# Fewer bytes from HBM, 16 more GpSimd copies: blocks of k doubled on the chip in a fused window-attention and MoE kernel

## Chip, cores and metric

The kernel runs on one core of one Trainium2 chip. The metric is device time in microseconds (us) for one launch; "profiled execution" is one launch that the hardware profiler recorded, and times inside it count from the start of its span.

## What is computed

```python
# attention: B, H, S, D = 8, 8, 576, 64; every token sees itself and the 63 tokens before it
scores = q @ k.transpose(0, 1, 3, 2) / sqrt(D)
scores = where((rel >= 0) & (rel < 64), scores, -1e9)        # rel = query position - key position
attn = softmax(scores, axis=-1)
x = (attn @ v)                                               # to N, D = 4608, 512
# MoE on x: E = 8 experts, F = 1024, only tokens with x @ w_skip > 0
gate_w, e = max, argmax of softmax(x @ w_gate)
out = x + gate_w * (relu(x @ w1[e]) @ w2[e])                 # other tokens: out = x
```

All arrays are f32.

## The kernel before

A sequence of 576 tokens is nine blocks of 64. A query block needs two key blocks: its own and the one before it. The work is cut into 36 tiles of 128 tokens, and a tile is two query blocks. For each pair m of batches (m = 0 to 3) there are nine tiles: eight with blocks 0 to 7 of the two batches, and as the ninth the "tail" tile 9m+8, the last blocks (block 8) of both batches.

Loads come in groups n = 0 to 15. A group is four blocks (two tiles) of one batch, g = n % 2 says which half of the batch. `first_of[n]` is the group's first tile (0, 2, 4, 6, 9, 11, 13, 15, 18, ...). k lies in four buffers `ks[n % 4]` of five blocks: slots 1 to 4 hold the group's blocks, slot 0 the block before the first one. In an even group slot 0 is zero, set once; in an odd group it is the last block of group n-1, and L209 loads it from HBM again, so that this transfer has five blocks. A tail tile has k tiles `kt` and q tiles `qt` of its own, loaded by `load_qk_tail` (L212) in four transfers, among them block 7 a second time (`kT[..., 7:9]`). v comes in two forms: `vT` for the router's logits, and `vm`, whose four blocks have two halves of partitions: the lower 64 partitions hold the block before, the upper 64 the block itself, or the other way round. `load_vm` (L298) fills every second block over all partitions, GpSimd (L356) and ScalarE (L363, L376) copy the other halves.

The main loop (L1163) is written out by hand under a manual schedule: every engine gets its instructions in the order of the program text. Iteration t does, in this order:

- what the table `at[t]` lists: loads on SP's queue with the memsets that belong to them on GpSimd (L305);
- `score(t+1)` on TensorE: four mask matmuls (L237) and 32 matmuls with q and k (L251), for a tail tile with `qt` and `kt`;
- the gate steps: `gate_v` (L335) and `gate_vt` with GpSimd's copy L356;
- `routes(1)`: one step of the router for a group of tiles (8, 8, 6, 6, 8 tiles). The steps for the first 28 tiles run on GpSimd: `pool_part` (L467 to L504), the ranks (L536 to L538), `one_hots` (L584 to L610), and when the third group is in, `close_first` (L625 to L648);
- softmax of tile t on VectorE (L270, L271) and ScalarE (L276);
- `tile_out(t-2)`: 32 matmuls with v on TensorE (L387), the division on VectorE (L398 to L406), and the store of tile t-4 on SP's queue (L425, L427). x has four buffers;
- two more `routes(1)`, between them the transposes of tile t-1 (L284).

`at[t]` is filled from L1142 on: first for all n (`load_qk` at `first_of[n]-5`, `load_v` at `first_of[n]-4`), then for all m (`load_qk_tail` at 9m+4, `load_v_tail` at 9m+2). So the tail tile 17 of m = 1 is scored in iteration 16, and the tail tile 26 of m = 2 in iteration 25. After the loop come the experts (L911 to L913), whose weights are split by ScalarE (L843) and VectorE (L847).

Of the kernel before, what the change touches and what calls it, by code (L numbers as in the profile page):

```python
# [8 lines left out]
F32 = mybir.dt.float32  # L9
# [9 lines left out]
B, H, S, HD = 8, 8, 576, 64  # L19
N, D, E, F = 4608, 512, 8, 1024  # L20
P = 128
# [27 lines left out]
NQB, NKB, NVB, NTB, NSB, NPB, XPB = 4, 4, 4, 2, 2, 3, 4  # L49
# [20 lines left out]
VW = 64 + 1 + 9  # L70
# [73 lines left out]
def window_attention_moe(ctx: ExitStack, tc, a, out):  # L144
    nc = tc.nc
# [42 lines left out]
    vp = attn.enter_context(tc.tile_pool(name="vp", bufs=2, side="right"))  # L188
# [4 lines left out]
    qkp = scoring.enter_context(tc.tile_pool(name="qkp", bufs=1))  # L193
# [3 lines left out]
    ks = [qkp.tile([P, 5, 4, 64], F32, name=f"k{s}") for s in range(NKB)]  # L197
    for k in ks[::2]:
        nc.gpsimd.memset(k[:, 0], 0.0)
    qs, tails = {}, {}  # L200

    def load_qk(n, parts=((0, 4),), other=nc.sync):
        b, g = divmod(n, 2)
        if parts[0][0] == 0:
            qs[n] = qkp.tile([P, 4, 4, 64], F32, name="q", bufs=NQB)
        q, k = qs[n], ks[n % NKB]
        for s, e in parts:
            s0 = s + 1 if s or not g else 0
            nc.sync.dma_start(k[:, s0 : e + 1], a["kT"][b, :, 4 * g + s0 - 1 : 4 * g + e])  # L209
            other.dma_start(q[:, s:e], a["qT"][b, :, 4 * g + s : 4 * g + e])  # L210

    def load_qk_tail(m):  # L212

        q = qkp.tile([P, 2, 4, 64], F32, name="qt")
        k = qkp.tile([P, 2, 2, 4, 64], F32, name="kt")
        for z in range(2):
            nc.sync.dma_start(k[:, z], a["kT"][2 * m + z, :, 7:9])
            nc.sync.dma_start(q[:, z], a["qT"][2 * m + z, :, 8])
        tails[m] = q, k

    def windows(t):

        m, r = divmod(t, 9)
        if r == 8:
            q, k = tails[m]
            return [(q[:, z], k[:, z]) for z in range(2)]
        n, j = 4 * m + r // 2, 2 * (r % 2)
        return [(qs[n][:, j + z], ks[n % NKB][:, j + z : j + z + 2]) for z in range(2)]

# [58 lines left out]
    ss, pts, vs = {}, {}, {}  # L288
    banks = {}
    vms = {}  # L290

    def load_vT(n):
        b, g = divmod(n, 2)
        vT = vtp.tile([P, 4, 256], F32, name="vT")
        nc.sync.dma_start(vT, a["vT"][b, g])
        vTs[n] = vT

    def load_vm(n, by=nc.sync):  # L298
        b, g = divmod(n, 2)
        vm = vp.tile([P, 4, H, VW], F32, name="vm", bufs=NVB)  # L300
        by.dma_start(
            vm.rearrange("p (j z) h c -> p j z (h c)", z=2)[:, :, 1], a["vp"][b, :, 2 * g : 2 * g + 2]
        )
        if g == 0:
            nc.gpsimd.memset(vm[:64, 0], 0.0)  # L305
        vms[n] = vm

    def load_v(n):
        load_vT(n)
        load_vm(n)  # L310
# [3 lines left out]
    def load_v_tail(m):  # L314
        vt = vp.tile([P, 2, H, VW], F32, name="vt", bufs=1)
        vT = vtp.tile([P, 4, P], F32, name="vTt", bufs=1)
        nc.sync.dma_start(vT, a["vTt"][m])
        for z in range(2):
            nc.sync.dma_start(vt[64:, z], a["vpt"][m, z])
        vms["t", m] = vt, vT  # L320

    def keep_busy(n):
# [17 lines left out]
    def gate_t(vw, nt):  # L340
        pk = psum.tile([P, nt, P], F32, name="pk", tag="t", bufs=2, padded_shape=[P, 4, P])
        for j in range(nt):
            nc.tensor.transpose(pk[:, j], vw[:, j * P : j * P + P], ident)
        return pk.rearrange("p n (h c) -> p n h c", c=16)[..., 0:9]
# [4 lines left out]
    def gate_vt(n):  # L349

        b, g = divmod(n, 2)
        vm = vms[n]
        pg = gate_t(vws.pop(n), 2)
        w = vm.rearrange("p (j z) h c -> p j z h c", z=2)
        nc.scalar.copy(w[:, :, 1, :, 65:74], pg)  # L355
        nc.gpsimd.tensor_copy(w[64:, :, 0], w[:64, :, 1])  # L356
        for j in range(2):
            vs[9 * (n // 4) + 2 * (n % 4) + j] = [vm[:, 2 * j], vm[:, 2 * j + 1]]

    def lower(n, j):  # L360

        before = vms[n][64:, 1] if j else vms[n - 1][64:, 3]
        nc.scalar.copy(vms[n][:64, 2 * j], before)  # L363

    def gate_tail(m):
        vms["t", m] = vms["t", m][0], gate(vms["t", m][1], 1)
# [6 lines left out]
        vs[9 * m + 8] = [vt[:, 0], vt[:, 1]]  # L373

    def tail_lower(m, z):
        nc.scalar.copy(vms["t", m][0][:64, z], vms[4 * m + 2 * z + 1][64:, 3])  # L376

    def av_tile(t, lh, sums, av=None):
        blks = tiles[t]
# [739 lines left out]
    first_of = [9 * (n // 4) + 2 * (n % 4) for n in range(NG)]  # L1119
    with tc.manual_schedule():  # L1120
        other = nc.scalar
        nc.vector.memset(onesb, 1.0)
        nc.sync.dma_start(identb, a["c_identb"])
        other.dma_start(band, a["c_band"])
        load_qk(0, ((0, 2),), other)
        load_qk(0, ((2, 4),), other)
        load_vT(0)
        other.dma_start(ident, a["c_ident"])
        other.dma_start(wg, a["wg"])
        nc.scalar.activation(sm.tile([P, 1], F32, name="warm", bufs=1), onesb[:, 0:1], AF.Exp)  # L1130
        load_qk(1, ((0, 2),), other)
        load_vm(0, other)
        load_qk(1, ((2, 4),), other)
        load_vT(1)
        load_vm(1)
        at = {}

        def when_at(t, f, n):
            at.setdefault(max(t, 0), []).append((f, n))

        gate_at, lower_at = {}, {}
        for n in range(NG):  # L1142
            if n >= 2:
                when_at(first_of[n] - AHEADQ, load_qk, n)
                when_at(first_of[n] - AHEADV, load_v, n)
            gt = max(first_of[n] - (1 if n < NSLOW else 2), 0)
            gate_at.setdefault(gt, []).append((gate_v, n))
            at_t = gt + 1
            gate_at.setdefault(at_t, []).append((gate_vt, n))
            lower_at.setdefault(at_t, []).append((lower, n, 1))  # L1150
            if n % 2:
                lower_at.setdefault(at_t + 1, []).append((lower, n, 0))
        for m in range(B // 2):
            when_at(9 * m + 4, load_qk_tail, m)
            when_at(9 * m + 2, load_v_tail, m)
            lower_at.setdefault(9 * m + 4, []).append((tail_lower, m, 0))
            lower_at.setdefault(9 * m + 7, []).append((tail_lower, m, 1))
            gate_at.setdefault(9 * m + 5, []).append((gate_tail, m))
            gate_at.setdefault(9 * m + 6, []).append((gate_tail_t, m))
# [3 lines left out]
        for t in range(NT - 1):  # L1163
            m, r = divmod(t, 9)
# [206 lines left out]
        while True:  # L1371
            k = place[0]
# [16 lines left out]
    with tc.If(more > 0):  # L1389
        with tc.For_i(0, more, 1) as i:  # L1390
# [15 lines left out]
            for qi in range(NQ):  # L1406
                both = []
                for w in range(2):
                    n = 2 * qi + w
# [15 lines left out]
def layout(inputs):  # L1425
    q, k, v = (np.asarray(inputs[n]) for n in "qkv")
    arr = {}
    for name, z in (("qT", q), ("kT", k)):
        z = z.reshape(B, 4, 2, NB, 64, HD)
        arr[name] = z.transpose(0, 2, 5, 3, 1, 4).reshape(B, P, NB, 4, 64)  # L1430
    vp = np.zeros((B, NB, 64, H, VW), np.float32)
    vp[..., HD] = 1.0
    vp[..., :HD] = v.reshape(B, H, NB, 64, HD).transpose(0, 2, 3, 1, 4)
    arr["vp"] = vp[:, :8].reshape(B, 4, P, H * VW).transpose(0, 2, 1, 3)
    arr["vpt"] = vp[:, 8].reshape(B // 2, 2, 64, H, VW)
    vb = v.reshape(B, 4, 2, S, HD).transpose(0, 2, 4, 1, 3).reshape(B, P, 4, S)
    arr["vT"] = vb[..., :512].reshape(B, P, 4, 2, 256).transpose(0, 3, 1, 2, 4)
    arr["vTt"] = vb[..., 512:].reshape(B // 2, 2, P, 4, 64).transpose(0, 2, 3, 1, 4).reshape(B // 2, P, 4, P)
    wg = np.zeros((2, HD, 4, 2, 16), np.float32)
    for z in range(2):  # L1440
        wg[z, :, :, z, :E] = inputs["moe_w_gate"].reshape(4, 2, HD, E)[:, z].transpose(1, 0, 2)
        wg[z, :, :, z, E] = inputs["moe_w_skip"].reshape(4, 2, HD)[:, z].T
    arr["wg"] = wg.reshape(P, 4, 32)
    w1 = inputs["moe_w1"].reshape(E, NDC, P, NQ, FQ).transpose(0, 3, 2, 1, 4).reshape(E, NQ, P, NDC * FQ)
    w2 = inputs["moe_w2"].reshape(E, NQ, 2, P, D).transpose(0, 1, 3, 2, 4).reshape(E, NQ, P, 2 * D)
    arr["wq"] = np.concatenate([w1, w2], 3).reshape(E * NQ * P, 2048)
    arr.update(constants())
    return {n: np.ascontiguousarray(x) for n, x in arr.items()}
# [17 lines left out]
```

## Time and profile before

| | |
|---|---|
| time, median of 3 (lowest, highest) | 418.26 us (417.87, 418.77) |
| profiled execution | 418.07 us |
| its span (the rest lies around it) | 416.3 us |
| TensorE (PE) busy, matmuls | 398.2 us, 96% |
| VectorE (DVE) busy | 291.6 us, 70% |
| ScalarE (ACT) busy | 219.4 us, 53% |
| GpSimd (POOL) busy | 157.6 us, 38% |
| DMA | 105.73 MB, mean 254 GB/s |

Attention fills the span to about 160 us, the experts the rest. A busy share is a mean over both: which engine holds up the others is read from the waits in a stretch. "[2.10 <-DMA q<-qT]" at the end of a line means that the engine was idle for 2.10 us before this instruction and that the q transfer ended last of what it waited for. PEclk is the clock granted to TensorE as a share of 2.4 GHz, so that 0.50 is the lower level of 1.2 GHz.

### The profile page before, as it was taken

The page shows a single profiled execution, that of the slowest core. Times are in us where ns is not written, and L with a number is a line of the kernel's source. Part 1 is how long each engine was busy: PE and PEld are TensorE (multiplying, and loading weights), DVE is VectorE, ACT ScalarE, POOL GpSimd, SP SyncE. Part 2 cuts the span into 40 slices and gives each one's busy share as a digit, 9 for nine tenths or more (in the row PEclk, how much of TensorE's full clock was granted, in tenths as well). Part 3 has the DMA queues.
Part 4 walks back from the last instruction along what each step waited for, and adds up shares of the span by engine and source line. Part 5 has one row for each costly group of instructions (what it writes and reads, how often), then busy time and mean ns, then how long its engine had stood idle before and what let it go on. Part 6 is the DMA issues. An engine that isn't in the chain of part 4 may idle for free.

```text
span 416.3 us, 11734 instructions
## 1 busy us (share of the span) xinstructions
PE 398.2 (96%) x4687; PEld 334.5 (80%) x4687; DVE 291.6 (70%) x515; ACT 219.4 (53%) x389; POOL 157.6 (38%) x296
## 2 busy tenths in 40 slices
PE   8699999999999889899999999999999999999994
PEld 3587887878778678779988898898888889988873
DVE  3387899899799797999436679555556485656661
ACT  2477868767767695436224436234426355444540
POOL 1431168666958878557103115013016030100110
PEclk9999999999999999899999999999999999999999
DMA  8999999999995695636928937545388866667810
GB/s 296 406 326 375 408 368 382 410 386 310 366 413 195 204 362 173 196 128 219 311 82 254 324 117 258 183 161 205 117 250 291 264 206 202 221 203 244 265 55 23
DMA packets 38554, 105.73 MB, mean 254 GB/s; under 512 B 4864, under 2 KB 6272, under 8 KB 38496
## 3 DMA queue, kind: packets, MB, share of 16 engines
q1 hardware_dynamic: 34016, 93.51, 65.3%
q0 software_dynamic: 3200, 9.58, 6.5%
q10 hardware_dynamic: 1280, 1.85, 1.2%
q8 instruction: 38, 0.62, 0.6%
q14 instruction: 20, 0.16, 0.1%
HBM read 90.86 MB, written 14.39 MB: 253 GB/s over the span
## 4 chain that ended last, share of the span: by engine, by line
PE 68%; DMA 10%; issue 7%; DVE 7%; POOL 4%; ACT 2%; POOLq 0%; ACTq 0%; DVEq 0%
PE av L387 8%; PE p L911 7%; PE p L912 7%; PE p L913 7%; PE pt L284 6%; PE ps L251 5%; DMA out<-yo,les 5%; PE yv L911 3%; PE yw L911 3%; PE yw L912 3%; PE yw L913 3%; PE yv L912 3%; PE yv L913 3%; DMA q<-qT 2%; PE ps L237 2%
## 5 line engine op out<-in xcount | busy, mean ns | idle before, releaser
L847 DVE TENSOR_TENSOR wlo<-raw,whi 128x1024 fp32r<-128x1024 f32 x70 | 85.6, 1233 | 17.5 <-ACT whi L843 17.5
L957 ACT ACTIVATE hh<-p 128x256 fp32r<-128x256 f32 (+6 forms) x72 | 27.7, 384 | 127.3 <-PE p L913 123.0
L911 PE MATMUL p<-xh,whi 128*128 128x256 f32 (+6 forms) x288 | 85.9, 298 | 0.2 <-DVE hl L960 0.2
L912 PE MATMUL p<-xl,whi 128*128 128x256 f32 (+6 forms) x288 | 84.3, 293 | 0.8 <-DVE xl L892 0.8
L913 PE MATMUL p<-xh,wlo 128*128 128x256 f32 (+6 forms) x288 | 84.4, 293 | 0.6 <-DVE wlo L847 0.6
L843 ACT CAST whi<-raw 128x1024 fp32r<-128x1024 f32 x72 | 74.3, 1046 | 0.0
L1003 POOL DMA_INDIRECT out<-yo,les x18 | 17.6, 976 | 147.3 <-DVE yo L994 137.6
L960 DVE SCALAR_TENSOR_TENSOR hl<-p,hh 128x256 fp32r<-128x256 f32 (+6 forms) x72 | 30.1, 419 | 61.2 <-ACT hh L957 35.5
L911 PEld LDWEIGHTS p<-xh,whi 128*128 128x128 f32 x288 | 55.2, 192 | 3.7 <-issue 1.7
L912 PEld LDWEIGHTS p<-xl,whi 128*128 128x128 f32 x288 | 55.3, 192 | 2.1 <-DVE xl L892 1.1
L913 PEld LDWEIGHTS p<-xh,wlo 128*128 128x128 f32 x288 | 55.4, 192 | 0.8 <-DVE wlo L847 0.8
L276 ACT ACTIVATE s<-s 128x1024 f32<-128x1024 f32 x36 | 38.1, 1058 | 30.9 <-DVE s L271 30.8
L270 DVE TENSOR_REDUCE mx<-ps 128x8 f32<-128x1024 f32 x36 | 43.6, 1210 | 6.1 <-PE ps L251 6.1
L271 DVE TENSOR_TENSOR s<-ps,mx 128x1024 f32<-128x1024 f32 x36 | 44.1, 1225 | 4.6
L387 PEld LDWEIGHTS av<-vm,ptm 128*64 128x64 f32 x992 | 35.2, 138 | 12.2 <-issue 5.5
L387 PE MATMUL av<-vm,ptm 128*64 128x74 f32 x992 | 40.4, 233 | 3.4 <-POOL vm L356 1.4
L285 ACT COPY ptm<-pt 128x512 f32<-128x512 f32 x72 | 38.3, 581 | 5.9 <-PE pt L284 5.8
L284 PE MATMUL pt<-ident,s 128*128 128x128 f32 x288 | 39.9, 283 | 0.0
L251 PE MATMUL ps<-k,q 64*64 64x128 f32 x1024 | 33.6, 270 | 2.5 <-DMA q<-qT 2.5
L251 PEld LDWEIGHTS ps<-k,q 64*64 64x64 f32 x1024 | 30.0, 133 | 5.3 <-issue 3.1
L284 PEld LDWEIGHTS pt<-ident,s 128*128 128x128 f32 x288 | 31.6, 143 | 2.5 <-issue 0.3
L356 POOL COPY vm<-vm 64x1184 f32<-64x1184 f32 x16 | 18.6, 1166 | 34.9 <-ACT vm L355 29.2
(225 smaller groups left out, 699.9 us busy)
## 6 DMA issues: line engine op xcount, KB each, us to landing
raw<-wq SPq DMA_DIRECT2D x72, 512.0 KB, 4.7
vm<-vp SPq DMA_DIRECT2D x15, 592.0 KB, 9.1
vT<-vT SPq DMA_DIRECT2D x16, 512.0 KB, 8.3
out<-x SPq DMA_DIRECT2D x32, 256.0 KB, 7.3
q<-qT SPq DMA_DIRECT2D x14, 512.0 KB, 9.1
wr<-wq SPq DMA_DIRECT2D x24, 256.0 KB, 5.5
k<-kT SPq DMA_DIRECT2D x7, 640.0 KB, 8.6
k<-kT SPq DMA_DIRECT2D x7, 512.0 KB, 8.7
```

What stands on the lines that cost most here:

```text
L251: nc.tensor.matmul(ps[64 * hf : 64 * hf + 64, r, p], q[h, p], k[h, :, p], start=False, stop=p == 3, skip_group_check=True,)
L270: nc.vector.tensor_reduce(mx, flat, axis=AX.X, op=ALU.max)
L271: pace[0] = nc.vector.tensor_tensor(s, flat, mx.unsqueeze(2).to_broadcast([P, 8, P]), op=ALU.subtract)
L276: nc.scalar.activation(s, s, AF.Exp, scale=0.125)
L284: nc.tensor.transpose(pt[:, p], s[:, 4 * r + p], ident)
L285: nc.scalar.copy(ptm[:, 4 * r : 4 * r + 4], pt)
L387: nc.tensor.matmul(av[64 * hf : 64 * hf + 64, h // 4, (h % 4) * VW : (h % 4 + 1) * VW], ptm[:, (h % 2) * 4 + h // 2, 64 * hf : 64 * hf + 6 ...
L843: nc.scalar.copy(ring[n % RING][0], raws[n % NRAW])
L847: by.tensor_tensor(lo, raws[n % NRAW], hi.bitcast(F32), op=ALU.subtract)
L911: nc.tensor.matmul(o, lh, rh, start=first, stop=False, skip_group_check=parts)
L912: nc.tensor.matmul(o, lh, rl, start=False, stop=False, skip_group_check=parts)
L913: nc.tensor.matmul(o, ll, rh, start=False, stop=last, skip_group_check=parts)
```

## The change

The blocks of q and k are no longer loaded twice. `kT` and `qT` hold blocks 0 to 7 only. A k transfer has four blocks for every group. Slot 0 of an odd group is copied by GpSimd from slot 4 of group n-1 (`last_block`, 128 x 256 f32, eight copies: one before the loop, seven from `at[first_of[n]-4]`). A tail tile gets one transfer of 512 KB with k and q of both last blocks into a tile of three parts, and GpSimd copies the two block-7 parts from `ks` (`last_block_tail`, 128 x 256 f32, eight copies: in `at[9m+4]` for group 4m+1 and in `at[9m+5]` for group 4m+3). They are entered after all n, so they stand behind the memset of the same iteration. `vm` is laid out by parity: the loaded blocks lie side by side, so a row of the transfer is one run of 4736 bytes in place of two of 2368. The two `vpt` transfers of a tail are one.

```diff
-            s0 = s + 1 if s or not g else 0
-            nc.sync.dma_start(k[:, s0 : e + 1], a["kT"][b, :, 4 * g + s0 - 1 : 4 * g + e])
+            nc.sync.dma_start(k[:, s + 1 : e + 1], a["kT"][b, :, 4 * g + s : 4 * g + e])
...
-        for z in range(2):
-            nc.sync.dma_start(k[:, z], a["kT"][2 * m + z, :, 7:9])
-            nc.sync.dma_start(q[:, z], a["qT"][2 * m + z, :, 8])
-        tails[m] = q, k
+        both = qkp.tile([P, 3, 2, 4, 64], F32, name="kqt")
+        nc.sync.dma_start(both[:, 1:3], a["kqt"][m])
+        tails[m] = both
+
+    def last_block(n):
+        nc.gpsimd.tensor_copy(ks[n % NKB][:, 0], ks[(n - 1) % NKB][:, 4])
+
+    def last_block_tail(n):
+        nc.gpsimd.tensor_copy(tails[n // 4][:, 0, n % 4 // 2], ks[n % NKB][:, 4])
...
-            return [(q[:, z], k[:, z]) for z in range(2)]
+            return [(tails[m][:, 2, z], tails[m][:, 0:2, z]) for z in range(2)]
...
-        vm = vp.tile([P, 4, H, VW], F32, name="vm", bufs=NVB)
+        vm = vp.tile([P, 2, 2, H, VW], F32, name="vm", bufs=NVB)
...
-        for z in range(2):
-            nc.sync.dma_start(vt[64:, z], a["vpt"][m, z])
+        nc.sync.dma_start(vt[64:], a["vpt"][m])
...
-        nc.gpsimd.tensor_copy(w[64:, :, 0], w[:64, :, 1])
+        nc.gpsimd.tensor_copy(vm[64:, 0], vm[:64, 1])
...
         load_qk(1, ((2, 4),), other)
+        last_block(1)
...
                 when_at(first_of[n] - AHEADV, load_v, n)
+                if n % 2:
+                    when_at(first_of[n] - 4, last_block, n)
...
             when_at(9 * m + 4, load_qk_tail, m)
+            when_at(9 * m + 4, last_block_tail, 4 * m + 1)
+            when_at(9 * m + 5, last_block_tail, 4 * m + 3)
```

## Rows read from the trace of the kernel before

**Rows 1.** Busy us and count of each engine in a stretch: PE, PEld, DVE, ACT, POOL.
```profile
60.00:80.00 20.00, 20.00 (x434) 16.00 (x422) 18.27 (x34) 15.61 (x29) 16.03 (x35) 1.00 1.03 379
```

**Rows 2.** The chain that ended last, in order of time: start, us, what.
```profile
8.23 8.80 DMA q<-qT
...
75.31 0.87 PE ps L251 x32
...
137.98 1.17 POOL vm L356
```

**Rows 3.** Timeline, TensorE: start, us, line, out<-in, [idle before <-releaser].
```profile
17.17 0.56 PE L251 MATMUL ps<-k,q 64*64 64x128 f32 x12 [2.10 <-DMA q<-qT]
```

**Rows 4.** DMA issues: queue, count, KB each, median us from issue to landing.
```profile
vm<-vp ACTq DMA_DIRECT2D x1, 592.0 KB, 9.0
k<-kT SPq DMA_DIRECT2D x1, 384.0 KB, 6.3
```

**Rows 5.** Windows as in rows 1; the last three columns: PEclk, DMA share, GB/s.
```profile
14.00:18.00 4.00, 1.85 (x44) 1.13 (x44) 0.47 (x1) 1.27 (x4) 1.96 (x3) 1.00 1.04 411
18.00:22.00 4.00, 4.00 (x53) 3.51 (x45) 1.24 (x5) 1.62 (x3) 3.94 (x9) 0.60 1.03 408
136.00:140.00 4.00, 2.57 (x68) 1.84 (x70) 2.64 (x4) 3.15 (x6) 3.78 (x6) 1.00 0.41 121
168.00:172.00 4.00, 2.00 (x18) 1.08 (x17) 4.00 (x10) 1.22 (x2) 1.47 (x2) 1.00 0.63 194
172.00:176.00 4.00, 3.96 (x20) 3.96 (x21) 3.36 (x12) 1.68 (x3) 1.76 (x8) 0.57 0.60 179
```

**Rows 6.** Timeline, GpSimd, its first long run without idle time.
```profile
67.65 0.20 POOL L591 CAST vals<-gl 128x8 bf16<-128x8 f32 x1
67.80 0.62 POOL L598 TENSOR_TENSOR xg<-cf,gc 128x256 f32<-128x256 f32 x1
...
73.97 2.47 POOL L610 TENSOR_TENSOR xg<-xg,vals 128x640 bf16<-128x640 f32 x2
76.39 0.58 POOL L305 MEMSET vm<- 64x592 f32 x1
77.03 1.17 POOL L356 COPY vm<-vm 64x1184 f32<-64x1184 f32 x1
```

**Rows 7.** Timeline, TensorE: the scores of tail tiles 17 and 26.
```profile
75.14 1.04 PE L251 MATMUL ps<-kt,qt 64*64 64x128 f32 x32
...
111.15 0.50 PE L251 MATMUL ps<-kt,qt 64*64 64x128 f32 x12
```

**Rows 8.** Timeline, GpSimd: small one-input instructions.
```profile
32.01 0.29 POOL L179 CAST trib<-cf 128x128 bf16<-128x128 f32 x1 [1.80 <-DMA cf<-c_f]
32.24 0.19 POOL L180 COPY base<-cf 128x8 f32<-128x8 f32 x1
```

**Rows 9.** Timeline, GpSimd: its second long run, and the idle time after it.
```profile
95.86 0.30 POOL L536 TENSOR_TENSOR gds<-gds,gohb 128x64 f32<-128x64 f32 x1 [2.01 <-DVE gds L529]
...
109.79 0.59 POOL L305 MEMSET vm<- 64x592 f32 x1
...
112.85 0.28 POOL L468 TENSOR_TENSOR lg<-lh 128x54 f32<-128x54 f32 x1
...
117.46 0.27 POOL L498 TENSOR_TENSOR goh<-gfi,gfm 128x48 f32<-128x48 f32 x1 [2.39 <-DVE gfm L492]
```

**Rows 10.** Timeline, VectorE, behind that run.
```profile
113.17 0.20 DVE L481 TENSOR_REDUCE gmx<-lg 128x6 f32<-128x48 f32 x1 [1.84 <-POOL lg L468]
```

**Rows 11.** Timeline, SP's queue: a k load and the store behind it.
```profile
102.90 0.92 SPq L209 DMA_DIRECT2D k<-kT  x1
...
104.54 0.45 SPq L425 DMA_DIRECT2D out<-x  x1
```

**Rows 12.** Timeline, the experts' stage: VectorE and GpSimd at the same time.
```profile
175.67 2.36 DVE L847 TENSOR_TENSOR wlo<-raw,whi 128x1024 fp32r<-128x1024 f32 x2
...
175.96 1.07 POOL L586 TENSOR_SCALAR gc<-gc 128x8 f32<-128x8 f32 x1
```

More of the change, by code (lines that the diff above doesn't have):

```diff
@@ L207, in load_qk @@
         for s, e in parts:
-            s0 = s + 1 if s or not g else 0
-            nc.sync.dma_start(k[:, s0 : e + 1], a["kT"][b, :, 4 * g + s0 - 1 : 4 * g + e])
+            nc.sync.dma_start(k[:, s + 1 : e + 1], a["kT"][b, :, 4 * g + s : 4 * g + e])
             other.dma_start(q[:, s:e], a["qT"][b, :, 4 * g + s : 4 * g + e])
     def load_qk_tail(m):
-        q = qkp.tile([P, 2, 4, 64], F32, name="qt")
-        k = qkp.tile([P, 2, 2, 4, 64], F32, name="kt")
-        for z in range(2):
-            nc.sync.dma_start(k[:, z], a["kT"][2 * m + z, :, 7:9])
-            nc.sync.dma_start(q[:, z], a["qT"][2 * m + z, :, 8])
-        tails[m] = q, k
+        both = qkp.tile([P, 3, 2, 4, 64], F32, name="kqt")
[5 more added lines that the diff above has]
+        nc.gpsimd.tensor_copy(tails[n // 4][:, 0, n % 4 // 2], ks[n % NKB][:, 4])
     def windows(t):
@@ L224, in windows @@
         if r == 8:
-            q, k = tails[m]
-            return [(q[:, z], k[:, z]) for z in range(2)]
+            return [(tails[m][:, 2, z], tails[m][:, 0:2, z]) for z in range(2)]
         n, j = 4 * m + r // 2, 2 * (r % 2)
@@ L299, in load_vm @@
         b, g = divmod(n, 2)
-        vm = vp.tile([P, 4, H, VW], F32, name="vm", bufs=NVB)
+        vm = vp.tile([P, 2, 2, H, VW], F32, name="vm", bufs=NVB)
         by.dma_start(
-            vm.rearrange("p (j z) h c -> p j z (h c)", z=2)[:, :, 1], a["vp"][b, :, 2 * g : 2 * g + 2]
+            vm[:, 1].rearrange("p j h c -> p (j h c)"),
+            a["vp"][b, :, 2 * g : 2 * g + 2].rearrange("p j c -> p (j c)"),
         )
         if g == 0:
-            nc.gpsimd.memset(vm[:64, 0], 0.0)
+            nc.gpsimd.memset(vm[:64, 0, 0], 0.0)
         vms[n] = vm
@@ L353, in gate_vt @@
         pg = gate_t(vws.pop(n), 2)
-        w = vm.rearrange("p (j z) h c -> p j z h c", z=2)
-        nc.scalar.copy(w[:, :, 1, :, 65:74], pg)
-        nc.gpsimd.tensor_copy(w[64:, :, 0], w[:64, :, 1])
+        nc.scalar.copy(vm[:, 1, :, :, 65:74], pg)
+        nc.gpsimd.tensor_copy(vm[64:, 0], vm[:64, 1])
         for j in range(2):
-            vs[9 * (n // 4) + 2 * (n % 4) + j] = [vm[:, 2 * j], vm[:, 2 * j + 1]]
+            vs[9 * (n // 4) + 2 * (n % 4) + j] = [vm[:, 0, j], vm[:, 1, j]]
     def lower(n, j):
-        before = vms[n][64:, 1] if j else vms[n - 1][64:, 3]
-        nc.scalar.copy(vms[n][:64, 2 * j], before)
+        before = vms[n][64:, 1, 0] if j else vms[n - 1][64:, 1, 1]
+        nc.scalar.copy(vms[n][:64, 0, j], before)
     def gate_tail(m):
@@ L375, in tail_lower @@
     def tail_lower(m, z):
-        nc.scalar.copy(vms["t", m][0][:64, z], vms[4 * m + 2 * z + 1][64:, 3])
+        nc.scalar.copy(vms["t", m][0][:64, z], vms[4 * m + 2 * z + 1][64:, 1, 1])
     def av_tile(t, lh, sums, av=None):
@@ L1430, in layout @@
         arr[name] = z.transpose(0, 2, 5, 3, 1, 4).reshape(B, P, NB, 4, 64)
+    last = np.stack([arr[name][:, :, 8] for name in ("kT", "qT")], 2)
+    arr["kqt"] = last.reshape(B // 2, 2, P, 2, 4, 64).transpose(0, 2, 3, 1, 4, 5)
+    for name in ("qT", "kT"):
+        arr[name] = arr[name][:, :, :8]
     vp = np.zeros((B, NB, 64, H, VW), np.float32)
@@ L1434, in layout @@
     arr["vp"] = vp[:, :8].reshape(B, 4, P, H * VW).transpose(0, 2, 1, 3)
-    arr["vpt"] = vp[:, 8].reshape(B // 2, 2, 64, H, VW)
+    arr["vpt"] = vp[:, 8].reshape(B // 2, 2, 64, H, VW).transpose(0, 2, 1, 3, 4)
     vb = v.reshape(B, 4, 2, S, HD).transpose(0, 2, 4, 1, 3).reshape(B, P, 4, S)
```

## The prediction, made before the changed kernel ran

> **What bounds the kernel now.** I read the stretches first, then the chain, then the queues of the engines that the change touches. In the middle of attention TensorE is busy without a gap (20.00 of 20 us), VectorE nearly so (18.27), GpSimd 16.03 [rows 1]. The chain agrees: it starts with a q transfer, runs over TensorE from 17 to 114 us, then over VectorE and, from 121 to 139 us, over GpSimd, whose copy of v at 137.98 releases TensorE [rows 2]. So bytes matter only at the start, TensorE's own time matters up to 114 us, and GpSimd's queue where it is late. The list of waits between 20 and 114 us has no transfer that TensorE, VectorE or ScalarE waited for.
>
> GpSimd is late twice. The memset at 76.39 belongs to iteration 14 (group 8) and waits for nothing, yet it stands right behind the router's work of iteration 13 [rows 6], while TensorE scores tile 17, which is iteration 16, at 75.14 [rows 7]. So GpSimd works its queue in the order of the text, some two iterations behind TensorE. The second time it has no idle time from 95.86 to 113.13 (112.85 + 0.28): the memset of iteration 23 stands at 109.79 [rows 9], TensorE scores tile 26 (iteration 25) at 111.15 [rows 7], and VectorE sits idle for 1.84 us until GpSimd's `lg` is there [rows 10].
>
> **The change part by part.** The sum is made against the profiled execution's 418.07 us (span 416.3, 1.8 around it). It lies 0.19 below the median of 418.26, inside the spread of 0.9, so I leave the sum as it is.
>
> *Bytes at the start.* k of group 1's first half shrinks from 384 to 256 KB [rows 4]. The transfers run at 411 GB/s with the DMA engines full [rows 5], so what queues behind lands 131 KB / 411 = 0.32 us earlier, and TensorE's wait of 2.10 us for q [rows 3] shrinks by as much: **-0.3**. Bounds: 0 (the transfers on ScalarE's queue don't pass on what SP's saves) and -2.1 (the wait goes altogether).
>
> *Other transfers.* Seven k loads lose 128 KB each, the tails 1 MB in all, and sixteen fewer DMAs are issued. All of it lies under TensorE's unbroken work [rows 1] and nobody waits for it: 0. Without that cover it would be some 2 MB / 411 = 5 us of DMA time. The longer runs of `vm` move the same bytes, and GpSimd copies as many elements as before in L356: 0; at the end of a long run of GpSimd a slower L356 would cost its own difference.
>
> *Price of one copy.* 128 x 256 f32 is not in the trace. One-input instructions take 0.19 for 8 elements a partition, 0.29 for 128 [rows 8], 1.17 for 1184 [rows 6]. The line from 8 to 1184 gives 0.19 + 248 x 0.83 ns = 0.40, and it goes through the point at 128. Bounds: 0.29 (half the elements) and 0.62 (two inputs, 128 x 256, L598 [rows 6]). From start to start add up to 0.07 (0.64 for the memset of 0.58 at 76.39 [rows 6]): 0.43.
>
> *Tail copies of m = 1.* `last_block_tail(5)` is in `at[13]`: in GpSimd's order between L591 (iteration 12) at 67.65 and L598 at 67.80, so all behind it shifts by 0.43. `last_block_tail(7)` is in `at[14]` behind the memset: it starts at 76.39 + 0.43 + 0.64 = 77.46 and ends at 77.86. Tile 17's matmuls with the second half's window need it, the third of the 32 first, at about 75.2 [rows 7]. TensorE's queue is in order: behind the waiting matmul stand the gate, AV of tile 14 and the transposes, and VectorE and ScalarE wait for these. The stretch has no gap that takes it up, so **+2.7** (77.86 + 0.04 for the hand-over - 75.2). Bounds by the copy's: 2.5 to 3.1. Both sides move alike when TensorE is earlier, since GpSimd's run began with VectorE's result of iteration 12.
>
> *The clock behind that wait.* With TensorE busy for 1.85 us of 14 to 18 its granted clock was 0.60 in the next 4 us, and with 2.00 of 168 to 172 it was 0.57, stretches at the lower of the two levels in both; with 2.57 of 136 to 140 it stayed [rows 5]. From 74 to 78 there would be 1.3 us of work. I take a drop: 4 x 0.40 = 1.6 or 4 x 0.43 = 1.7, **+1.7**, on the engine that bounds this stretch. Bounds 0 and 2.0.
>
> *Tail copies of m = 2.* `at[22]` and `at[23]` put two copies around the memset at 109.79, in a run without idle time whose end VectorE awaits [rows 9, 10]: `lg` is later by 2 x 0.43 to 0.47, **+0.9** (bounds 0.6 to 1.3). VectorE runs without a pause from 113.17 to 121.2, hands over to GpSimd's next run, and that ends in the copy at 137.98 on the chain [rows 2]. TensorE's own wait for the second copy is small (109.79 + 0.43 + 0.64 + 0.40 = 111.26 against 111.2 [rows 7]) and not the one that ends last.
>
> *The other copies of `last_block`.* Each has three iterations (some 12 us) before its score. Those of iterations 20 and 25 fall before the idle 2.01 and 2.39 us of [rows 9]; the one of iteration 29 and the tail copies of 31 and 32 stand behind the copy at 137.98, and their readers (scores of tiles 33 and 35) are over 2 us later. I take 0; if the run from 142 to 169 us passes them on, up to +0.5. At the start the copy waits for the second half of group 0's k, with only a memset behind it.
>
> *New waits on SP's queue.* The load of group 13's k (buffer 1, `at[24]`), issued at 102.90 [rows 11], overwrites what `last_block_tail(9)` reads, so it now waits for GpSimd until 109.79 + 0.40 = 110.2. The q load, a store, vT and vm queue behind it for 7.3 us. The store at 104.54 [rows 11] frees the x buffer that VectorE fills again at 120.2; issued at 111.5 and landed 7.3 us later (the median of these stores) it is there at 118.8. vT of group 13 would be there at about 119, its gate is at 121.6. Hidden, with 1.4 to 2.6 us to spare: 0, and if not, up to +3.
>
> Sum: -0.3 + 2.7 + 1.7 + 0.9 = +5.0, so 418.07 + 5.0 = **423.1 us**.
>
> **The rivals.**
> *No drop of the clock* (0.15): as above without 1.7: 421.4. For it: the stall is one piece, and TensorE is fully busy on both sides. Against: less work in the 4 us than before either drop [rows 5].
> *The start gives back more* (0.06). vm of group 0 (592 KB on ScalarE's queue, landed after 9.0 us [rows 4]) has half as many runs now. If queues take turns run by run, q behind it lands some 1 us earlier, 14 to 18 us is busier and the clock stays up there: -1.1 - 1.6 in place of -0.3, 420.7. The Trainium skill, "DMA: Bandwidth & Descriptors", section "Queues, rings and completion order", says that a DMA engine goes round the queues packet by packet; by that rule alone q gains this only if SP's runs beside it don't grow too, and SP's vm, which shares those turns, does grow. The landing times before (vm 15.5, q 17.0, SP's vm 16.5) don't decide it.
> *GpSimd's copies are slowed by VectorE* (0.04). In the experts' stage an instruction on 8 elements a partition took 1.07 us beside L847 [rows 12], where a copy of that size took 0.19 [rows 8]. If the tail copies were slowed by as much (0.9 each), the wait grows by 1.8 and the second run by 1.8: 426.7. Against: the L356 copies took 1.16 to 1.17 us all sixteen times in attention. The Trainium skill, "GPSIMD Engine Reference", section "Key points", says that GpSimd shares its interfaces with VectorE and contends with instructions of two SBUF inputs; L847 is one, attention's large ones read PSUM, so by the rule too the copies stay at their price.
> *SP's stall is not covered* (0.07). It decides as soon as landing takes over 9 us or the copy of iteration 22 is over 1.4 us later than worked out: VectorE then waits for x, up to 3 us: 426.
> *Not slower* (0.08): the tail copies are in time. The point from which it decides is 75.2 us: `last_block_tail(7)` must stand before the run of [rows 6], where its input has long landed, that is, the order of the text must not hold on GpSimd, or the run must be 2.7 us shorter. Then the second run takes them likewise, and the start alone is left: 417.8; with more from the start 416. Against: the memset at 76.39, which had nothing to wait for.
>
> **How the numbers follow.** Forecast (stall, drop, second run) 0.60, and the rivals as given. The predicted time is the forecast's, 423.1. Its own range is 422.1 to 424.6. The range reaches down over "no drop" and "the start gives more" with their bounds, 420.0, and up over part of SP's stall, 425.8; left out are "not slower" and most of the two upper rivals, under 0.2. A measurement of this kernel can tell about 0.2% (0.84 us) from no change. Faster (below 417.4) only in a part of "not slower": 0.03; same 0.06; slower 0.91.
>
> **What would show it.** In the trace after: TensorE idle for 2.5 to 3 us at the first matmuls of tile 17's scores (about 75 us), released by a GpSimd copy; granted clock near 0.6 in the 4 us behind; copies of 0.4 us; VectorE's wait for `lg` 0.9 longer than 1.84; the wait for q near 17 us shorter by 0.3; SP's k load of group 13 issued only after the copy of iteration 22. The prediction is wrong if the copies stand elsewhere in GpSimd's order, if TensorE doesn't stop at tile 17, or if a part of the stall is made up before 139 us.

## The result, and the profile after

The changed kernel took 423.12 us (median of six runs, 421.17 to 425.72) beside 417.77 for the kernel before (417.24 to 418.77): a ratio of 1.0130, 95% interval 1.0095 to 1.0164. A later measurement, beside the kernels of the second group of experiments, gave 1.0167 (1.0135 to 1.0199), so the change costs 5 to 7 us. The profiled execution took 423.74 us (span 422.0), 5.7 us over that of before.

The page after shows what the change does to the transfers: 103.63 MB in place of 105.73, and 34458 packets in place of 38554. GpSimd is busy for 163.5 us in place of 157.6.

```profile
DMA packets 34458, 103.63 MB, mean 246 GB/s; under 512 B 4608, under 2 KB 4992, under 8 KB 34400
```

The list of waits of TensorE, 12 to 145 us (in all, how often, the longest), shows the new wait for `kqt`. The line "issue" is TensorE standing still with no releaser in the profile.

```profile
PE av L389 <- issue: 3.8, 2, 2.0
PE ps L254 <- DMA q<-qT: 2.4, 2, 2.0
PE ps L254 <- POOL kqt L223: 2.2, 1, 2.2
PE av L389 <- POOL vm L358: 1.3, 1, 1.3
```

**Tile 17.** The timeline of TensorE, and that of GpSimd beside it. After four matmuls with the first half's window, TensorE stands until the second tail copy of m = 1, which GpSimd makes behind its long run, has ended [compare rows 6, 7]. The gate that follows begins at 80.14 (76.12 before), so 2.6 of the 4.0 us between the traces arise here; 1.4 were there already.

```profile
76.31 0.41 PE L240 MATMUL ps<-band,identb 64*64 64x512 bf16 x4
76.55 0.38 PE L254 MATMUL ps<-kqt 64*64 64x128 f32 x4
79.12 1.09 PE L254 MATMUL ps<-kqt 64*64 64x128 f32 x28 [2.19 <-POOL kqt L223]
80.14 0.64 PE L338 MATMUL pw<-vT,wg 128*32 128x256 f32 x8
```

```profile
69.19 0.40 POOL L223 COPY kqt<-k 128x256 f32<-128x256 f32 x1
...
75.72 2.47 POOL L612 TENSOR_TENSOR xg<-xg,vals 128x640 bf16<-128x640 f32 x2
78.14 0.58 POOL L309 MEMSET vm<- 64x592 f32 x1
78.67 0.39 POOL L223 COPY kqt<-k 128x256 f32<-128x256 f32 x1
79.13 1.17 POOL L358 COPY vm<-vm 64x1184 f32<-64x1184 f32 x1
```

**The clock behind it.** Windows of the same trace, columns as in [rows 1, 5]. TensorE works 2.9 us of each of these 4 us and keeps the full clock.

```profile
74.00:78.00 4.00, 2.93 (x49) 2.26 (x48) 3.67 (x8) 3.12 (x7) 4.00 (x6) 1.00 1.01 358
78.00:82.00 4.00, 2.88 (x69) 2.22 (x70) 1.16 (x1) 1.51 (x3) 2.63 (x5) 1.00 1.02 414
```

**GpSimd's second run.** From 99.89 to the start of `lg` it takes 17.68 us, before 16.99 [rows 9]: 0.69 longer, for two copies.

```profile
99.89 0.31 POOL L538 TENSOR_TENSOR gds<-gds,gohb 128x64 f32<-128x64 f32 x1 [1.55 <-DVE gds L531]
...
113.82 0.41 POOL L223 COPY kqt<-k 128x256 f32<-128x256 f32 x1
114.16 0.59 POOL L309 MEMSET vm<- 64x592 f32 x1
114.69 0.40 POOL L223 COPY kqt<-k 128x256 f32<-128x256 f32 x1
115.15 1.17 POOL L358 COPY vm<-vm 64x1184 f32<-64x1184 f32 x1
117.57 0.29 POOL L470 TENSOR_TENSOR lg<-lh 128x54 f32<-128x54 f32 x1
```

VectorE, which waits for `lg`, does not wait longer in this trace: 0.39 us, where it was 1.84 before [rows 10]. TensorE had stood for 1.80 us near 107 us (shown below under "The start"), so VectorE came to `lg` later itself.

```profile
117.89 0.20 DVE L483 TENSOR_REDUCE gmx<-lg 128x6 f32<-128x48 f32 x1 [0.39 <-POOL lg L470]
```

**SP's queue.** k of group 13 is issued 10.6 us behind the instruction ahead of it, once GpSimd has made the copy of iteration 22 [compare rows 11]. No wait of TensorE, VectorE or ScalarE for a transfer appears between 100 and 145 us.

```profile
103.62 0.34 SPq L427 DMA_DIRECT2D out<-x  x1
114.26 0.33 SPq L208 DMA_DIRECT2D k<-kT  x1
```

**The start.** TensorE's wait for q looks unchanged: 1.98 us in place of 2.10 [rows 3]. But it ends 1.6 us later, at 18.77. In the trace of before the clock fell behind this wait (0.60 from 18 to 22 us [rows 5]), in this one it did not; so both reach the score at 22.6 us at the same time, and the pair of traces hides that the start had changed.

```profile
18.77 1.10 PE L254 MATMUL ps<-k,q 64*64 64x128 f32 x32 [1.98 <-DMA q<-qT]
...
35.66 0.28 PE L389 MATMUL av<-vm,ptm 128*64 128x74 f32 x1 [2.02 <-issue]
...
107.58 0.73 PE L389 MATMUL av<-vm,ptm 128*64 128x74 f32 x14 [1.80 <-issue]
```

By this one pair, the traces are 1.4 us apart when TensorE comes to tile 17 (1.3 of it is the longer stall near 35 us, which has no releaser), 4.0 behind the wait, 4.7 at `lg` (117.57 against 112.85) and 5.1 at the copy of v at 137.98 [rows 2], here 143.04; the stall near 107 us adds nothing at `lg`. The experiments show that the stalls belong to no part of the change, and that the start, which this pair counts at nothing, costs about as much as the wait.

### The profile page after: what moved, and what is told of

It is laid out like the page before. It is cut to its first block, busy times and chain, and to the rows that moved or that the text cites. A ratio compares the mean times of both kernels' runs of the same rounds, so it can differ in the third digit from the quotient of the medians.

```text
span 422.0 us, 11737 instructions
## 1 busy us (share of the span) xinstructions
PE 398.4 (94%) x4687; PEld 333.4 (79%) x4687; DVE 292.0 (69%) x515; ACT 220.1 (52%) x389; POOL 163.5 (39%) x312
## 2 busy tenths in 40 slices
DMA packets 34458, 103.63 MB, mean 246 GB/s; under 512 B 4608, under 2 KB 4992, under 8 KB 34400
## 3 DMA queue, kind: packets, MB, share of 16 engines
q10 hardware_dynamic: 1152, 1.85, 1.4%
## 4 chain that ended last, share of the span: by engine, by line
PE 60%; DMA 13%; POOL 9%; issue 9%; DVE 6%; ACT 2%; POOLq 0%; ACTq 0%; DVEq 0%; SPq 0%
PE p L913 7%; PE p L915 7%; PE p L914 7%; PE av L389 6%; DMA out<-yo,les 5%; PE pt L287 4%; PE ps L254 4%; PE yv L913 3%; DMA vm<-vp 3%; PE yw L913 3%; PE yw L914 3%; PE yv L914 3%; PE yw L915 3%; PE yv L915 3%; POOL xg L604 2%
```

## The experiments

Each ratio is to the kernel before, run beside it on the same chip, with its 95% interval; before took 421.17 us in the first group, 418.42 in the second and 418.01 in the third. The expectations of the first group give times that were set against some 418 us, so its results are compared as ratios: 421.5 us, above which theory B of early1 lies, is 1.008.

### First group: which part of the change costs

**early1**: the tail copies of m = 1 are made in iteration 11, ahead of GpSimd's long run.

```
-            when_at(9 * m + 4, last_block_tail, 4 * m + 1)
-            when_at(9 * m + 5, last_block_tail, 4 * m + 3)
+            if m in (1,):
+                when_at(9 * m + 2, tail_tile, m)
+                when_at(9 * m + 2, last_block_tail, 4 * m + 1)
+                when_at(9 * m + 2, last_block_tail, 4 * m + 3)
+            else: ...
```

> The two tail copies of m = 1 stand two and three iterations earlier on GpSimd (both in iteration 11, where it is idle); all else as changed. Theory A (the wait at tile 17 is the main cost): that wait goes from the trace, the time falls by 2.5 to 2.7 us, and by some 1.7 more if the clock drops behind that wait in most executions: 418.8 to 420.6. Theory B (the new transfers cost it, by a later start and by stalls of TensorE for which the profile names no releaser): the time stays above 421.5. Theory C (GpSimd's second long run and SP's stall carry most of it): falls by less than 1.

1.0080 (1.0057 to 1.0103). The wait at tile 17 is gone from the trace, but the ratio lies above the 418.8 to 420.6 us of theory A (1.002 to 1.006) and at the edge of theory B's.

**early12**: the same for m = 2 (`if m in (1, 2)`).

> As early1, and the tail copies of m = 2 both in iteration 20, ahead of GpSimd's second long run; SP's load of group 13 then finds its copy done. Theory A: 0.7 us below early1, that is 418.0 to 419.9. Theory B: above 421. Theory C: 3 us or more below early1.

1.0085 (1.0051 to 1.0119). So theory A falls as an account of the whole: with the copies of m = 1 and m = 2 early, 0.85% (3.6 us) stays. And it is no faster than early1 (425.03 us against 424.56), where theory A wanted 0.7 us less: these times do not show what the late copies of m = 2 cost.

**v_only**: the kernel before with v's new layout and the one transfer of `vpt`, nothing on k and q.

> The kernel before with v laid out by parity and v's last blocks in one transfer, nothing else. Theory A: no change, 417.4 to 418.2. Theory B: slower by 1 to 3 us, with a stall of TensorE without a named releaser of 1 to 2 us that the kernel before has not, or a start that is later by over 1 us.

1.0018 (0.9997 to 1.0039): at most a small part of it, and not to be told from nothing.

**unread**: the kernel before with the eight tail copies at their places in the order, from `ks` into a buffer that nobody reads then.

```
+    def unread_copy(n):
+        nc.gpsimd.tensor_copy(raws[5][:, :256].rearrange("p (h c) -> p h c", c=64), ks[n % NKB][:, 4])
...
+            when_at(9 * m + 4, unread_copy, 4 * m + 1)
+            when_at(9 * m + 5, unread_copy, 4 * m + 3)
```

> The kernel before with eight more GpSimd copies at the places of the tail copies, from the same blocks of k into memory that nobody reads: GpSimd's longer queue and SP's new wait without TensorE's wait. Theory A: no wait at tile 17, second run longer by 0.7: +0.7, 418.3 to 418.7. Theory C: +3 or more. Theory B: no change.

1.0020 (0.9999 to 1.0042), some 0.8 us, as theory A has it, though the time alone can't be told from nothing. GpSimd's second run is 17.75 us long, and VectorE's wait for `lg` grows from 1.84 us [rows 10] to 2.69:

```profile
114.02 0.20 DVE L484 TENSOR_REDUCE gmx<-lg 128x6 f32<-128x48 f32 x1 [2.69 <-POOL lg L471]
```

What is left after early12 is in what the first group did not touch: k's and q's transfers, and the other copies. The windows from 3 to 8 us (last columns: granted clock, DMA share, GB/s) of the kernel before, of the changed kernel and of early12 show it:

```profile
3.00:8.00 5.00, 5.00 (x52) 2.21 (x54) 0.89 (x1) 1.49 (x2) 0.00 (x0) 1.00 1.03 382
```

```profile
3.00:8.00 5.00, 5.00 (x45) 2.17 (x44) 0.01 (x1) 1.49 (x2) 0.00 (x0) 1.00 0.87 226
```

```profile
3.00:8.00 5.00, 5.00 (x47) 2.14 (x46) 0.34 (x1) 1.49 (x2) 0.00 (x0) 1.00 0.92 229
```

The first transfers, k and q of group 0, are the same in size and order in all of these; v_only and unread move 377 and 378 GB/s. The transfers differ only in where they read: the host now leaves out the ninth block of each row, so a partition's row in DRAM is 8192 bytes long in place of 9216. That is theory P of the next expectations.

### Second group: the pitch of k and q in DRAM

**after2**: the changed kernel again.

> The changed kernel again, beside the kernels of this call and with a second trace. In the runs so far the changed kernel and its two variants moved 226 to 229 GB/s from 3 to 8 us, the kernel before, the one with v's layout alone and the one with unread copies 377 to 382. Theory P (k and q now lie in rows of 8192 bytes a partition in DRAM, before of 9216, and transfers of 2 KB pieces out of such rows are slow at the start): 220 to 235 GB/s from 3 to 8 us again, TensorE's wait for q of tile 3 ends between 18 and 20 us, 1.008 to 1.014 of the kernel before. Theory L (the late copies of tile 17 are all there is, the start varies from run to run): the start of this trace may be at 380 GB/s. Both expect a wait of 2 to 2.3 us for kqt at tile 17. Theory F (stalls of TensorE inside AV with no named releaser belong to the change): one of 1.5 us or more near 105 to 108 us again; if it is chance, none there.

1.0167 (1.0135 to 1.0199), above theory P's 1.008 to 1.014; 217 GB/s from 3 to 8 us, and tile 3's wait for q ends at 18.98, as theory P has it. The same wait at tile 17, again with no fall of the clock behind it (1.00 from 78 to 86 us), and no stall near 105 us: theory F falls, that stall was of the one execution.

```profile
80.21 1.09 PE L254 MATMUL ps<-kqt 64*64 64x128 f32 x28 [2.19 <-POOL kqt L223]
```

```profile
78.00:82.00 4.00, 1.81 (x44) 1.21 (x44) 2.12 (x2) 1.51 (x4) 3.73 (x6) 1.00 1.02 416
82.00:86.00 4.00, 4.00 (x90) 3.34 (x88) 2.69 (x6) 3.42 (x6) 0.00 (x0) 1.00 1.04 407
```

**pad9**: the changed kernel, rows of nine blocks in DRAM as before, the ninth not read.

```
-    for name in ("qT", "kT"):
-        arr[name] = arr[name][:, :, :8]
```

> The changed kernel with k and q kept in rows of nine blocks (9216 bytes) in DRAM as before; the ninth block isn't read from there. Nothing else differs, the transfers have the same sizes and the same order. Theory P: 375 to 385 GB/s from 3 to 8 us, TensorE's wait for q of tile 3 ends between 16.3 and 17.3 us, 1.5 to 2.5 us faster than the changed kernel, 1.006 to 1.008 of the kernel before. Rival (the copy at the start, or the smaller first transfer of group 1, slows the start): 226 GB/s as in the changed kernel and no difference of time.

1.0096 (1.0061 to 1.0131), 3.0 us below after2; 371 GB/s (theory P: 375 to 385), and the wait for q ends at 16.86. The rival falls. The gain is somewhat more than theory P wanted (1.5 to 2.5 us), and yet the ratio stays above its 1.006 to 1.008.

```profile
3.00:8.00 5.00, 5.00 (x48) 2.17 (x46) 0.78 (x1) 1.49 (x2) 0.93 (x2) 1.00 1.00 371
```

```profile
16.86 1.10 PE L254 MATMUL ps<-k,q 64*64 64x128 f32 x32 [1.64 <-DMA q<-qT]
```

In this execution the clock does fall behind tile 17's wait, by 4 x 0.16 + 4 x 0.26 = 1.7 us. On the timeline TensorE takes 5.59 us from the end of the wait to the scores of the next tile (81.78), where it took 4.04 in both traces of the changed kernel: 1.55 us lost.

```profile
76.19 1.52 PE L254 MATMUL ps<-kqt 64*64 64x128 f32 x28 [1.89 <-POOL kqt L223]
```

```profile
74.00:78.00 4.00, 2.11 (x40) 1.38 (x38) 2.40 (x3) 1.73 (x3) 3.71 (x6) 0.84 1.00 398
78.00:82.00 4.00, 4.00 (x60) 3.02 (x56) 1.29 (x5) 2.22 (x4) 0.00 (x0) 0.74 0.79 259
```

**early12_pad9**: early12 and pad9 together.

> Tail copies of m = 1 and m = 2 early (iterations 11 and 20) and rows of nine blocks in DRAM. If the late copies (2.1 us by the first of these runs) and the row pitch (P: 2 us) are the whole of the loss, this is within 0.3% of the kernel before, 1.000 to 1.003 with 1.0018 for v's layout. If something else of the change costs (theory F, stalls of TensorE with no named releaser, 1 to 3 us): 1.004 or more.

1.0001 (0.9982 to 1.0020), 418.11 us: within 0.2% the two causes are the whole loss. Tile 17's scores run without a wait, and GpSimd's run to `lg` takes 17.01 us again.

```profile
74.44 1.04 PE L257 MATMUL ps<-kqt 64*64 64x128 f32 x32
```

**pitch8**: the kernel before, only that k and q lie in rows of eight blocks; the tails read the last blocks from an array of their own.

```
-            nc.sync.dma_start(k[:, z], a["kT"][2 * m + z, :, 7:9])
-            nc.sync.dma_start(q[:, z], a["qT"][2 * m + z, :, 8])
+            nc.sync.dma_start(k[:, z], a["kl"][2 * m + z])
+            nc.sync.dma_start(q[:, z], a["ql"][2 * m + z])
...
+    arr["kl"] = arr["kT"][:, :, 7:9]
+    arr["ql"] = arr["qT"][:, :, 8]
+    for name in ("qT", "kT"):
+        arr[name] = arr[name][:, :, :8]
```

> The kernel before, with k and q in rows of eight blocks (8192 bytes) in DRAM and the last blocks, which the tails load, in an array of their own; transfers, order and copies as before. Theory P: 220 to 240 GB/s from 3 to 8 us, TensorE's wait for q of tile 3 ends 1.5 to 2.5 us later than the 17.2 of before, 1.004 to 1.006 of the kernel before. Rival (the start of the changed kernel is slow for another reason): 380 GB/s and 1.000 within 0.2%.

1.0059 (1.0042 to 1.0076): the loss appears in the kernel before, with no copy and none of the new transfers. The wait for q ends at 18.28, 1.1 us later than in the trace of before; the theory had 1.5 to 2.5.

```profile
3.00:8.00 5.00, 4.18 (x46) 1.95 (x45) 0.14 (x1) 1.49 (x2) 0.00 (x0) 1.00 0.92 239
```

```profile
18.28 1.99 PE L251 MATMUL ps<-k,q 64*64 64x128 f32 x32 [1.26 <-DMA q<-qT]
```

### Third group: the sizes of the terms

**early1_pad9**: early1 with rows of nine blocks, so of the late copies only those of m = 2 are left.

> Tail copies of m = 1 early (iteration 11), those of m = 2 late as in the changed kernel, rows of nine blocks in DRAM. It stands beside the kernel of the last call with both early, which took 1.0001 of the kernel before. Theory G2 (GpSimd's second long run carries its two copies to TensorE's AV of tile 29): GpSimd's run from iteration 21 to lg is 17.9 to 18.0 us long in place of 17.3, and the time is 1.0015 to 1.0025 of the kernel before. Rival (the run's end isn't what the following work waits for): the run is as long, and the time is 1.000 within 0.1%.

1.0016 (0.9993 to 1.0038), 0.6 us over early12_pad9, from two groups. The times alone don't tell it from nothing. The trace shows the longer run: GpSimd's run to `lg` takes 17.69 us, 0.68 more than in early12_pad9, and VectorE waits 0.67 us longer (2.63 in place of 1.96). The run's length is the surer of the two. It is 17.68 to 17.75 us in the seven traces with these two copies in it and 16.98 to 17.05 in the seven without, while VectorE's wait is 0.39 to 2.69 us in the first seven and 0.94 to 2.00 in the others.

```profile
114.63 0.20 DVE L486 TENSOR_REDUCE gmx<-lg 128x6 f32<-128x48 f32 x1 [2.63 <-POOL lg L473]
```

```profile
112.78 0.20 DVE L486 TENSOR_REDUCE gmx<-lg 128x6 f32<-128x48 f32 x1 [1.96 <-POOL lg L473]
```

**longwait**: pad9 with the copy that tile 17 waits for made three times.

```
+        for _ in range(3 if n == 7 else 1):
             nc.gpsimd.tensor_copy(tails[n // 4][:, 0, n % 4 // 2], ks[n % NKB][:, 4])
```

> Rows of nine blocks, all copies late, and the copy that tile 17 waits for is made three times (the second and third write the same again): GpSimd is 0.8 us longer before it lets TensorE go on. Beside the same kernel with one copy (1.0096 of the kernel before, a granted clock of 0.84 and 0.74 from 74 to 82 us in its trace). Theory W (the wait is on the path at its full length): 0.8 us slower, 1.0115. Theory C (with a longer wait the granted clock falls in more of the executions): 0.8 and up to 1 us more, 1.0115 to 1.014, single runs at a mean clock of 0.98 to 0.985 in most, and the trace shows a clock under 0.9 somewhere from 74 to 84 us. Rival (the wait has slack, its end is not what counts): no slower than 1.0096.

1.0126 (1.0085 to 1.0166), 0.0030 or 1.3 us over pad9. The wait is 3.11 us, and the clock stands at the lower of its two levels for all of 78 to 82 us:

```profile
78.36 1.97 PE L255 MATMUL ps<-kqt 64*64 64x128 f32 x28 [3.11 <-POOL kqt L224]
```

```profile
74.00:78.00 4.00, 1.25 (x15) 0.76 (x13) 3.31 (x5) 2.65 (x4) 3.88 (x7) 0.89 1.03 413
78.00:82.00 4.00, 3.64 (x48) 2.50 (x50) 0.00 (x0) 0.57 (x2) 1.87 (x3) 0.50 0.76 308
82.00:86.00 4.00, 4.00 (x71) 3.44 (x68) 2.33 (x5) 2.46 (x4) 0.00 (x0) 0.75 0.74 228
```

That is 4 x (0.11 + 0.50 + 0.25) = 3.4 us of clock, of which a part fell while TensorE still waited. From the end of the wait to the scores of the next tile (84.95) it takes 6.59 us, 2.55 more than the 4.04 of the changed kernel. The intervals of longwait and pad9 overlap, so the times alone do not exclude slack. That the wait costs time is shown by pad9 beside early1_pad9, whose intervals lie apart; that it counts at its full length is not shown. 1.3 us fits theory C (0.8 to 1.8) and, with this noise, theory W; only the trace speaks for C.

**pitch10**: the kernel before with rows of ten blocks.

```
+        arr[name] = np.zeros((B, P, NB + 1, 4, 64), np.float32)
+        arr[name][:, :, :NB] = z.transpose(0, 2, 5, 3, 1, 4).reshape(B, P, NB, 4, 64)
```

> The kernel before with k and q in rows of ten blocks (10240 bytes a partition) in DRAM; the tenth is zero and never read. Rows of nine blocks gave 371 to 382 GB/s from 3 to 8 us, rows of eight 217 to 239, at 2 KB pieces. Theory P2 (8192 is slow for being a power of two): 360 to 385 GB/s and 1.000 within 0.15% of the kernel before. Rival P1 (rows of nine blocks are fast for being an odd number of KB, all even ones are slow): 210 to 300 GB/s and 1.003 to 1.006.

0.9994 (0.9970 to 1.0019), 377 GB/s. Rows of 10240 bytes are as fast as those of 9216, so it is not that the length is even in KB. It is one length that is slow, 8192 bytes; that it is slow for being a power of two is not shown. A whole array grows with its rows, so how far k and q lie from each other in DRAM changes with them; no run separates the two.

```profile
3.00:8.00 5.00, 5.00 (x46) 2.13 (x45) 0.18 (x1) 1.49 (x2) 0.00 (x0) 1.00 0.99 377
```

**konly**: early12_pad9 with v laid out, loaded and copied as in the kernel before.

```
-        vm = vp.tile([P, 2, 2, H, VW], F32, name="vm", bufs=NVB)
+        vm = vp.tile([P, 4, H, VW], F32, name="vm", bufs=NVB)
...
-        nc.gpsimd.tensor_copy(vm[64:, 0], vm[:64, 1])
+        nc.gpsimd.tensor_copy(w[64:, :, 0], w[:64, :, 1])
```

> The part of the change on k and q alone, with the tail copies of m = 1 and 2 early and rows of nine blocks; v is laid out and loaded as in the kernel before. Theory (late copies, pitch and 0.2% for v's layout are the whole loss; 0.3 us of the start are won back): 0.998 to 1.000 of the kernel before, the one that may beat it. Rival (v's layout costs nothing, and its 1.0018 was chance): as with v's layout, 1.000.

0.9983 (0.9957 to 1.0008), 417.33 us, the fastest of the group, yet not to be told from the kernel before. v's layout cost 0.0018 in both comparisons (v_only against before, and early12_pad9 against konly, from two groups), some 0.8 us; neither comparison alone tells that from nothing, and where it would arise stays open.

## Why the prediction was right, and where it was not

The total was predicted at +5.0 us and measured at +5.3, then +6.8. The wait for the late copy was there as worked out, but that the total came so close is in part luck: two errors of opposite sign, the start (3.3 us too low) and the clock (some 1 us too high), which do not even cancel, and a first measurement 1.5 us below the second.

*Where the late copy stands, and its price: right.* GpSimd works in the order of the text, `last_block_tail(7)` stands behind the long run, and a copy takes 0.39 to 0.41 us (predicted 0.40). The wait added 2.6 us in the trace of the changed kernel (predicted 2.7).

*The clock behind that wait: the step that failed is "I take a drop" as a sure term.* Of the four traces with this wait the clock fell in two (pad9, 1.55 us lost, and longwait, with a longer wait, 2.55) and stayed in two (the changed kernel, twice). In the ten traces without it the clock stayed at 1.00 from 74 to 82 us. The prediction read the drop off the work in 4 us (1.85 and 2.00 before a drop, 2.57 before none [rows 5]); in after2 TensorE worked 1.81 us of 78 to 82 and the clock stayed at 1.00 to 86 us, so that reading does not decide it. The size, 1.7, was about right where the drop came in pad9. Wait and clock together cost 0.0096 - 0.0016 = 0.0080, or 3.3 us (pad9 against early1_pad9, from two groups), where 4.4 were predicted; 3.3 - 2.6 leaves 0.7 for the clock on average, an estimate that the two intervals leave open by some 1.7 us either way. The rival "no drop" and the forecast both came true, from one execution to the next. The single times fit that, though a mean over the span doesn't tell where the clock fell: pad9's three at a mean clock of 0.980 to 0.982 took 422.36 to 423.89 us, its three at 0.990 to 0.993 took 419.45 to 421.79.

*Tail copies of m = 2: the run grew, somewhat less than forecast; its price in time is not shown.* Predicted 0.9; GpSimd's run is longer by 0.7 in the traces of the changed kernel and of early1_pad9 and, as copies that nobody reads, by 0.8 in that of unread. The times give 0.6 and 0.8 us (early1_pad9 against early12_pad9, unread against before), but early12 against early1 gives none. The step that was mis-sized is the 0.43 and 0.47 from start to start: the first copy takes 0.34 up to the memset (113.82 to 114.16), the memset 0.53 up to the second copy in place of 0.65 up to L356 before, and the second copy 0.46.

*Bytes at the start: wrong in sign.* The step was right in its arithmetic (0.32 us of bytes fewer) and put at nothing what the change also does to the source: it cuts the row from 9 blocks to 8. The transfers at the start are then paid at 217 to 239 GB/s for 5 us in place of 370 to 382. At 382 - 226 = 156 GB/s for 5 us, 0.78 MB less has arrived, which takes another 1.9 us at 406 GB/s (the rate of before from 8 to 20 us). That is what the traces show: tile 3's scores get their q between 18.10 and 19.68 us in the five traces with rows of 8192 bytes and between 16.37 and 17.42 in the nine others (means 18.76 and 16.86). TensorE's clock also fell in four of the five traces between 10 and 26 us, against two of the nine. At the third AV the means are 28.87 and 26.50 us, 2.4 apart. By the times the pitch costs 2.5 us (pitch8), 3.0 (after2 against pad9) and 3.5 (early12 against early12_pad9, from two groups). The rival "the start gives back more" looked at the same place in the wrong direction. The forecast's own 0.3 us of gain can't be seen by itself in any run.

*SP's new wait and the other copies: right.* The queue stood for 10.6 us (forecast: 7.3), and no engine waited for what stood behind it. With the tail copies of m = 1 and m = 2 early and the row long again, the rest of the change costs nothing that can be measured (early12_pad9, 1.0001).

Measured terms: start +3.0, wait and clock +3.3, GpSimd's second run +0.7, together +7.0; the changed kernel took +6.8 beside the kernels that gave the first of these. These terms are differences along one chain of kernels, from the changed one over pad9 and early1_pad9 to early12_pad9, so that they add up is no proof; what bears them out from outside the chain is pitch8 (+2.5 in the kernel before). "Not slower" fell for the reason given against it. The prediction's own list of signs was half blind: it asked whether the wait for q shrinks, and 1.98 against 2.10 seemed to say almost so, while the wait ended 1.6 us later. And it asked for a wait of VectorE for `lg` that is 0.9 longer, which the trace of the changed kernel does not show (0.39), although GpSimd's run had grown.

## What to carry to other kernels

When an edit drops a part of an array in DRAM, look at what the distance between partitions becomes, not only at the bytes: here rows of 8192 bytes cost 2.5 to 3.5 us at the start, and padding them back took it away. When a copy on the chip replaces a transfer, look up what its engine is doing at the point of the text where the copy is put: made two or three iterations earlier, ahead of GpSimd's long runs, and with the rows padded, the copies cost nothing that could be measured (1.0001). The change then saved nothing measurable either: most of its 2.1 MB lay under TensorE's unbroken work [rows 1]. And compare when a wait ends, in several traces, before believing that a wait of the same length is the same wait.

## What was not expected of the hardware

**Row pitch.** The first loads of k and q are pieces of 2 KB a partition (two blocks), on two queues, with loads of vT and others behind them. Out of rows of 8192 bytes the DMA engines moved 217, 226, 228, 229 and 239 GB/s in all from 3 to 8 us in five traces; out of rows of 9216 or 10240 bytes, 370 to 382 in nine. The Trainium skill, "DMA: Bandwidth & Descriptors", section "Latency and other measured facts", has a row on it: for copies between HBM tensors with 16 KiB a partition, row pitches of large powers of two lower the rate (207 GB/s at 512 KiB, 164 at 2 MiB, 103 at 4 MiB), and 4 KiB of padding restore it (214); aliasing of memory channels is named there as an inference. In that row the loss is nearly gone at 512 KiB; these runs, from DRAM to SBUF, show one at a pitch of 8 KiB, with 1 KiB of padding as the cure, so there they differ from the trend of the row. None shows the mechanism, and a pitch of 16384 bytes was not tried. The later loads of four blocks (4 KB pieces out of the same rows), mixed with other transfers, do not show it: from 20 to 60 us the changed kernel moved 380 GB/s, the kernel before 376.

```profile
20.00:60.00 40.00, 37.87 (x780) 30.10 (x779) 32.51 (x57) 28.67 (x50) 15.13 (x30) 1.00 1.03 380
```

**Stalls with no releaser.** One matmul of AV near 32 to 37 us waits with nothing named in every trace, for 0.46 to 2.17 us (0.73 before, 2.02 and 1.74 in the changed kernel, 2.17 in early1_pad9). It goes with no part of the change, and its cause stays open.
